# Products on a tile of ones around the first scores, queries scaled by immediates, and a later first output-weight block

## The chip, the cores and the metric

The kernel runs on one core of a Trainium2 chip. The metric is the device time of one execution, in microseconds (us). Before the change it is 948.71 us, the median of three runs (946.57 to 950.64).

## What is computed

Three layers, one after the other. First, attention over 4 batches of 8 heads, 576 positions, 64 values a head, with a causal window of 128 and a slope for each head:

```python
scores = scale * np.matmul(q, k.transpose(0, 1, 3, 2))
mask = (rel >= 0) & (rel < window)
scores = np.where(mask, scores + bias[None], -1000000000.0)
scores = scores - np.max(scores, axis=-1, keepdims=True)
attn = np.exp(scores)
attn = attn / (np.sum(attn, axis=-1, keepdims=True) + 1e-09)
attn_out = np.matmul(attn, v)
```

Its output, laid out as 2304 tokens of 512 values, goes through a gated layer of width 1536 (`silu(x @ w_gate) * (x @ w_val) @ w_out`) and then through a layer of width 2048 (`h * tanh(softplus(h)) @ w_out`, with `h = x @ w_in`).

## The kernel before

The 2304 tokens are cut into five chunks (512, 384, 512, 512, 384; `A_CHUNKS`). Attention of chunk c+1 is woven into the gated layer of chunk c; attention of chunk 0 stands alone, at the start. The last layer runs after all of that, with weights in seven combinations, and is not touched.

Only TensorE's order is written out by hand (`tc.manual_schedule(engines={PE})`): it is the order in which the program makes its calls. The order on VectorE (DVE), ScalarE (ACT), GpSimd (POOL) and on the DMA queue (SP) is made by a scheduler from its own estimates, so an edit in one place can move instructions of these engines far from it.

In chunk 0 a head h goes through these steps. **S(h)**, the scores (`score`, `mm` at L116): four products of queries by keys for the four blocks of 128 queries, two in each of two PSUM banks. They take 64 rows of the array, float32, and the profile shows each product as two instructions. DVE then puts the two diagonal halves together (L231, L238), adds the bias and takes the maximum (L245), and ACT takes exponentials and their sums (L249). `norm` adds a small number to the sums (L257), takes reciprocals (L260) and scales the weights, two blocks on ACT (L264) and two on DVE (L266). **T(h)**, four transposes (L271), which ACT copies (L277) and POOL masks (L280, L284). **O(r)**, for the pair r of heads 2r and 2r+1: weights by values into a bank, of which ACT and DVE make a high and a low part (L123, L126). The scores of a pair need its queries scaled first (`split`, L195: one ACT instruction for both heads, with a column of the constants `cst_sb` as scale).

TensorE's order is S(0), S(1), S(2), T(0), S(3), T(1), S(4), O(0), T(2), S(5) and so on. Scores, transposes, outputs and the hidden products `g_ps` of the gated layer take turns in four PSUM banks (tag `rot`); a product waits until the reader of the bank's last content is done.

Weights come as 64-bit patterns and are converted on the chip. `stage_w1(i)` loads raw block i of the first gated weight (tile `wst`, 1 MB; w0, w1, w2, ... below), `stage_other` raw block r of the output weight (tile `wraw`, 1 MB, one buffer; o0, o1, o2 below). `convert` makes five steps of each: one on ACT (`cg`, L434) and four on DVE (`cw` L446, `cp` L439, L451, L460). A w block is then split into halves, one on ACT (L123) and one on DVE (L126). These steps lie in a list, and `pump` hands them out between the pieces of attention. The first loads are issued in the order of `CFG["early"]`, where "w0", "w1", "w2" stand for the three entries of `stages`.

The gated layer of chunk 0 begins inside the attention (`begin`), and goes on after O(3): for block i a gate product and a tanh (L686, ACT), a product on DVE (L687), a value product, and h(i) (L697, DVE).

Of the kernel before, what the change touches and what calls it, by code (L numbers as in the profile page):

```python
# [9 lines left out]
F32 = mybir.dt.float32  # L10
F32R = mybir.dt.float32r
BF16 = mybir.dt.bfloat16
# [3 lines left out]
AF = mybir.ActivationFunctionType  # L16
# [5 lines left out]
F1, F2 = 1536, 2048  # L22
NF1, NF2 = F1 // 128, F2 // 128
W = 128
PLAIN = 3
CT = DM // 128
A_CHUNKS = [512, 384, 512, 512, 384]
# [66 lines left out]
def body(ctx: ExitStack, tc: tile.TileContext, qT, kT, vP, w1, w1o, w2, cst, yT):  # L94
# [20 lines left out]
    def mm(out, lhsT, rhs, start, stop):  # L115
        nc.tensor.matmul(out=out, lhsT=lhsT, rhs=rhs, start=start, stop=stop, skip_group_check=True)  # L116
# [12 lines left out]
    t = 0  # L129
# [2 lines left out]
        t += n  # L132


    x_t = {}

    def attention(ap, p, ci, s_native, upfront):
# [52 lines left out]
        def split(h):  # L190
            c = -float(2.0 ** (h - 2))
            if s_full(h):
                if h % 2 == 0:
                    q, k = raw.pop(h)
                    nc.scalar.activation(out=q, in_=q, func=AF.Copy, scale=qsc[:, h // 2:h // 2 + 1])  # L195
                    for e in range(2):
                        qk[h + e] = (q[64 * e:64 * e + 64], k[64 * e:64 * e + 64])
                return
            q, k = raw.pop(h)
            Q = ap.tile([128, p.n], F32R, tag="Q", name="Q")  # L200
            K1 = ap.tile([128, p.nk], F32R, tag="K1", name="K1")
            KL = ap.tile([128, p.nk], F32R, tag="KL", name="KL")
            nc.scalar.activation(out=Q, in_=q, func=AF.Copy, scale=c)
            hi_act(K1, k)
            nc.vector.scalar_tensor_tensor(
                out=Q[64:128], in0=q[64:128], scalar=c, in1=Q[64:128].bitcast(F32), op0=ALU.mult, op1=ALU.subtract
            )
            lo_dve(KL, k, K1)
            qk[h] = (Q, K1, KL)
# [105 lines left out]
    def attention_pieces(atts):  # L315

        heads = [(a, h) for a in atts for h in range(H)]
        pairs = [(a, r) for a in atts for r in range(HP)]
        n = len(heads)
        out = []  # L320

        def run(k, f):
            a, h = heads[k]
            return getattr(a, f)(h)

        def load(k):
            if not heads[k][0].upfront:
                run(k, "load")

        def load_v(r):  # L330
            if not pairs[r][0].upfront:
                pairs[r][0].load_v(pairs[r][1])

        def first():
            if atts[0].upfront:
                for c, i in ((x[0], int(x[1])) for x in CFG["early"]):
                    {"q": lambda: run(2 * i, "load"), "v": lambda: atts[0].load_v(i), "w": lambda: early[i]()}[c]()
            load(0)
            load_v(0)
            run(0, "split")  # L340
            load(1)
            load_v(1)

        def s_piece(k, g):
            a, h = heads[k]

            def f():
                if k == 0 and g == 0:
                    first()
                a.score(h, g)  # L350
                if g == a.ns - 1:
                    a.norm(h)
                    if k + 1 < n:
                        run(k + 1, "split")
                        if k + 2 < n:
                            load(k + 2)

            return (a.ci, 1.7 if a.s_full(h) else 0.87, f)

        def o_piece(k):  # L360
            a, h = heads[k]

            def f():
                if a.ci not in x_t:
                    x_t[a.ci] = xp.tile([128, 2, CT, 512], F32R, tag="x", name="xt")
                a.outp(h // 2)
                r = a.ci * HP + h // 2 + 2
                if r < len(pairs):
                    load_v(r)

            return (a.ci, a.nk * 0.46, f)

        def t_piece(k):
            a, h = heads[k]
            apart = 2.6 if h == H - 1 and a.ci == len(plansA) - 1 else 0.0
            return (a.ci, 0.48 + apart, lambda: a.transp(h))

        def delay(k):
            return CFG["delay0"] if heads[k][0].ci == 0 else 1

        for st in range(n + 4):
            todo = {"S": [], "T": [], "O": []}
            if st < n:
                todo["S"] = [s_piece(st, g) for g in range(heads[st][0].ns)]
            for k in range(max(0, st - 4), min(st, n)):
                if k + delay(k) == st:
                    todo["T"].append(t_piece(k))
                if k + delay(k) + 1 == st and heads[k][1] % 2 == 1:
                    todo["O"].append(o_piece(k))
            for c in CFG["order"]:  # L390
                if todo[c]:
                    out.append(todo[c].pop(0))
            for c in "SOT":
                out += todo[c]
        out.sort(key=lambda x: x[0] > 0)
        return out
# [88 lines left out]
    def stage_w1(i):  # L485
        stage[i] = (wp if i in (0, 1, 4, 5) else wq).tile([128, 2048], I32, tag="w", name="wst")
        nc.sync.dma_start(out=stage[i], in_=w1[i].bitcast(I32))

    def stage_other(key, src):
        stage[key] = bpool["a"].tile([128, 2048], I32, tag="wraw", name="wraw", bufs=1)  # L490
        nc.sync.dma_start(out=stage[key], in_=src.bitcast(I32))

    def conv_w1(i):
        st = {}

        def put(w):
            wt[i] = w
            stage.pop(i)
            if i + 4 < NF1:
                stage_w1(i + 4)  # L500

        def w_tile():
            return (wp if i < NF1 // 2 else wq).tile([128, 2, 1024], F32R, tag="w", name="w")

        steps(("w", i), convert(stage[i], st) + halves(st, w_tile, put))
# [480 lines left out]
    with tc.manual_schedule(engines={mybir.EngineType.PE}):  # L986
        spare = hp_.tile([128, 512], F32, tag="t", name="spare")[:, :1]
        nc.vector.memset(spare, 0.0)
        nc.scalar.activation(out=spare, in_=spare, func=AF.Exp)
        last = len(plansA) - 1  # L990
        att = tc.tile_pool(name="att", bufs=1, side="right")
        ap0 = att.__enter__()
# [19 lines left out]
        pieces = collections.deque(pieces)  # L1012
        lasts = [max(j for j, x in enumerate(pieces) if x[0] == ci) + 1 for ci in range(len(plansA))]
        at = 0
        stages = [lambda: stage_w1(0), lambda: stage_other(("o", 0), w1o[0]), lambda: stage_w1(1)]
        early.update(enumerate(stages))
        while at < lasts[0]:
            pieces.popleft()[2]()
            at += 1
            if at == 1:  # L1020
                conv_w1(0)
                conv_ring(0)
                conv_w1(1)
                nst = len(bg)
                stage_w1(2)
                stage_w1(3)
                behind.extend([last_of["max"], last_of["sum"]])
            if at == 4:
                behind.clear()
            f = (at / lasts[0] - CFG["conv_a"]) / (CFG["conv_b"] - CFG["conv_a"])  # L1030
            while bg and nst - len(bg) < f * nst:
                pump(1)
# [142 lines left out]
```

## Time and profile before

| | us |
|---|---|
| median of 3 runs | 948.71 |
| lowest, highest | 946.57, 950.64 |
| profiled execution, own time | 945.47 |
| profiled execution, span | 943.7 |
| TensorE busy | 919.4 |
| DVE busy | 701.4 |
| ACT busy | 519.7 |
| POOL busy | 204.7 |

A timeline row gives the start, the time from the first start to the last end of the merged instructions, the engine, the line, the operation, what it writes and reads, and how many instructions were merged; in brackets how long the engine stood idle before and what ended that. Matmuls of one row overlap, so a row's time divided by its count is the spacing. "PEclk" is the granted TensorE clock as a share of full speed; its record begins 42 us into the span, and before that the column shows full speed whatever was granted, so there the level is read from the spacing of the products.

### The profile page before, as it was taken

How to read it: one execution, taken by the hardware profiler on the slowest of the kernel's cores; microseconds unless marked ns; L12 is line 12 of the kernel's file. 1: busy time of each engine (PE TensorE's matmuls, PEld its weight loads, DVE VectorE, ACT ScalarE, POOL GpSimd, SP SyncE). 2: the span in 40 equal slices, each digit the busy share in tenths (PEclk: the TensorE clock that was granted, in tenths of full speed). 3: DMA queues.
4: the chain of work that ended last, by engine and by line, in shares of the span. 5: the costliest groups of instructions: out<-in, count | busy, mean ns of one | idle time of the engine just before them, and what ended most of it. 6: DMA issues, size and time to landing. Idle time of an engine off the chain costs nothing. (4 is left out here: it accounts for less than half of the span.)

```text
span 943.7 us, 14543 instructions
## 1 busy us (share of the span) xinstructions
PE 919.4 (97%) x5016; PEld 820.6 (87%) x5016; DVE 701.4 (74%) x1333; ACT 519.7 (55%) x1127; POOL 204.7 (22%) x332
## 2 busy tenths in 40 slices
PE   5999999999999999999999999999999999999998
PEld 4766678999988888888888999999999999999997
DVE  6898996687866865567665986887977878777673
ACT  6865667666575655445534554554535545355442
POOL 1312231111210332010013345551013410131000
PEclk9999999999999999999999999999999999999999
DMA  9855443376636464175437985426792267930375
GB/s 350 288 216 180 145 130 99 106 223 196 212 110 203 157 193 128 47 211 160 156 123 277 381 288 213 185 68 221 242 311 96 67 200 252 311 108 1 112 260 185
DMA packets 76729, 174.86 MB, mean 185 GB/s; under 512 B 8944, under 2 KB 52336, under 8 KB 66928
## 3 DMA queue, kind: packets, MB, share of 16 engines
q1 hardware_dynamic: 76512, 173.67, 55.3%
q8 instruction: 40, 0.66, 0.3%
q14 instruction: 33, 0.27, 0.1%
q10 hardware_dynamic: 144, 0.26, 0.1%
HBM read 138.25 MB, written 35.65 MB: 184 GB/s over the span
## 5 line engine op out<-in xcount | busy, mean ns | idle before, releaser
L116 PE MATMUL g_ps<-xt,w 128*128 128x512 f32 (+1 forms) x1440 | 318.3, 373 | 0.0
L116 PEld LDWEIGHTS g_ps<-xt,w 128*128 128x128 f32 x1440 | 257.6, 188 | 36.7 <-issue 3.5
L116 PE MATMUL bk<-xs,win 128*128 128x384 f32 x1008 | 177.9, 335 | 4.9 <-DVE G L759 4.6
L116 PEld LDWEIGHTS bk<-xs,win 128*128 128x128 f32 x1008 | 174.6, 188 | 7.8 <-DVE G L759 7.2
L116 PE MATMUL bk<-op,wout 128*128 128x384 f32 x1008 | 175.9, 334 | 1.3 <-DMA wout<-w2o 1.3
L116 PEld LDWEIGHTS bk<-op,wout 128*128 128x128 f32 x1008 | 174.7, 188 | 2.0 <-issue 2.0
L116 PE MATMUL acc<-hh,ring 128*128 128x512 f32 (+1 forms) x432 | 132.2, 369 | 0.0
L123 ACT ACTIVATE op<-G 128x768 fp32r<-128x768 f32 x84 | 71.0, 846 | 64.9 <-PE bk L116 64.8
L126 DVE TENSOR_TENSOR op<-G,op 128x768 fp32r<-128x768 f32 x84 | 80.2, 959 | 26.9 <-ACT op L123 24.9
L280 POOL TENSOR_SCALAR_AFFINE_SELECT PT<-PT 128x256 f32<-128x256 f32 (+4 forms) x80 | 43.2, 555 | 229.9 <-ACT PT L277 229.7
L850 POOL TENSOR_TENSOR t<-w 128x256 f32<-128x256 f32 x48 | 44.6, 950 | 210.1 <-issue 113.9
L116 PEld LDWEIGHTS acc<-hh,ring 128*128 128x128 f32 x432 | 80.0, 188 | 9.9 <-ACT hh L123 0.4
L116 PE MATMUL acc<-hl,ring 128*128 128x512 f32 (+1 forms) x216 | 79.0, 366 | 0.0
L249 ACT ACTIVATE Pt<-Pt,sm 128x128 f32<-128x128 f32 (+1 forms) x160 | 62.4, 391 | 16.1 <-DVE sm L245 15.7
L759 DVE TENSOR_TENSOR G<-u,bk 128x384 f32<-128x384 f32 x72 | 39.1, 553 | 36.6 <-PE bk L116 35.7
L1119 ACT ACTIVATE G<-G 128x384 f32<-128x384 f32 x72 | 37.0, 521 | 48.9 <-DVE G L759 48.9
L686 ACT ACTIVATE t<-g_ps 128x512 f32<-128x512 f32 (+1 forms) x60 | 32.9, 548 | 45.2 <-PE g_ps L116 45.1
L123 ACT ACTIVATE hh<-t 128x512 fp32r<-128x512 f32 (+1 forms) x54 | 31.2, 579 | 44.2 <-DVE t L702 44.0
L687 DVE SCALAR_TENSOR_TENSOR t<-t,g_ps 128x512 f32<-128x512 f32 (+1 forms) x60 | 37.6, 627 | 23.8 <-ACT t L686 23.7
L264 ACT ACTIVATE Pt<-Pt,sm 128x128 f32<-128x128 f32 (+1 forms) x144 | 46.3, 391 | 10.3 <-DVE sm L260 10.1
L126 DVE TENSOR_TENSOR hl<-t,hh 128x512 fp32r<-128x512 f32 (+1 forms) x54 | 36.6, 677 | 16.0 <-ACT hh L123 15.2
L759 DVE TENSOR_TENSOR G<-G 128x768 f32<-128x768 f32 x48 | 47.5, 990 | 0.8
(84 smaller groups left out, 1259.6 us busy)
## 6 DMA issues: line engine op xcount, KB each, us to landing
wout<-w2o SPq DMA_DIRECT2D x42, 1024.0 KB, 6.6
wraw<-w SPq DMA_DIRECT2D x16, 1024.0 KB, 5.5
w2o<-chl SPq DMA_DIRECT2D x16, 896.0 KB, 8.3
wst<-w SPq DMA_DIRECT2D x12, 1024.0 KB, 7.9
cw<-w1od SPq DMA_DIRECT2D x24, 512.0 KB, 4.5
w<-w2d SPq DMA_DIRECT2D x24, 512.0 KB, 3.3
w2d<-cw SPq DMA_DIRECT2D x16, 512.0 KB, 4.6
wraw<-w1o SPq DMA_DIRECT2D x6, 1024.0 KB, 6.9
```

The lines of the kernel that those rows point to most:

```text
L116: nc.tensor.matmul(out=out, lhsT=lhsT, rhs=rhs, start=start, stop=stop, skip_group_check=True)
L123: return nc.scalar.activation(out=out, in_=in_, func=AF.Copy)
L126: return nc.vector.tensor_tensor(out=out, in0=in_, in1=hi.bitcast(F32), op=ALU.subtract)
L249: last_of["sum"] = nc.scalar.activation(out=Pt[:q.qn], in_=Pt[:q.qn], func=AF.Exp, scale=-1.0, bias=sm[:q.qn, i:i + 1], accum_out=sm[:q.qn ...
L264: last_of["exp"] = nc.scalar.activation(out=pt, in_=pt, func=AF.Copy, scale=r)
L280: nc.gpsimd.affine_select(out=here, in_=prev, pattern=[[0, m], [1, n]], compare_op=ALU.is_ge, fill=0.0, base=0, channel_multiplier=-1,)
L686: tanhs.append(nc.scalar.activation(out=t[:, :n], in_=st["g"][:, :n], func=AF.Tanh, scale=0.5))
L687: nc.vector.scalar_tensor_tensor(out=t[:, :n], in0=t[:, :n], scalar=1.0, in1=st["g"][:, :n], op0=ALU.add, op1=ALU.mult)
L759: nc.vector.tensor_tensor(out=out, in0=a, in1=b, op=op)
L850: nc.gpsimd.tensor_tensor(out=x[:, o], in0=a, in1=b, op=ALU.subtract)
L1119: nc.scalar.activation(out=out, in_=in_, func=AF.Mish)
```

## The change

Four edits:

1. `runup(n)` issues n products of a 128x128 piece of a tile of bfloat16 ones by 128x512 of it, into the bank of tag `acc0`; nothing reads the result. 12 stand ahead of all scores, 4 behind the scores of each of heads 0, 1 and 2 (`RUNUP`). The tile is filled by one DVE memset.
2. The queries of heads 0 and 1 are scaled by constants written into the instructions: head 0's half on ACT, head 1's half on DVE, without the tile of constants.
3. In the early loads, w1 and o0 change places.
4. In the list of conversion steps, w1 comes ahead of o0.

```diff
+RUNUP = [12, 4, 4, 4]
...
+    def runup(n):
+        if not run:
+            t = hp_.tile([128, 512], F32, tag="t", name="ones")
+            run["one"] = t.bitcast(BF16)[:, :512]
+            nc.vector.memset(run["one"], 1.0)
+        spare = ps.tile([128, 512], F32, tag="acc0", name="spare", bufs=1)
+        for _ in range(n):
+            mm(spare, run["one"][:, :128], run["one"], True, True)
...
-                    nc.scalar.activation(out=q, in_=q, func=AF.Copy, scale=qsc[:, h // 2:h // 2 + 1])
+                    if upfront and h == 0:
+                        nc.scalar.activation(out=q[:64], in_=q[:64], func=AF.Copy, scale=c)
+                        nc.vector.tensor_scalar(out=q[64:], in0=q[64:], scalar1=2 * c, scalar2=None, op0=ALU.mult)
+                    else:
+                        nc.scalar.activation(out=q, in_=q, func=AF.Copy, scale=qsc[:, h // 2:h // 2 + 1])
...
                 a.score(h, g)
+                if g == a.ns - 1 and k + 1 < len(RUNUP):
+                    runup(RUNUP[k + 1])
...
         nc.scalar.activation(out=spare, in_=spare, func=AF.Exp)
+        runup(RUNUP[0])
...
-        stages = [lambda: stage_w1(0), lambda: stage_other(("o", 0), w1o[0]), lambda: stage_w1(1)]
+        stages = [lambda: stage_w1(0), lambda: stage_w1(1), lambda: stage_other(("o", 0), w1o[0])]
...
                 conv_w1(0)
+                conv_w1(1)
                 conv_ring(0)
-                conv_w1(1)
```

What moves is shown below as each kernel's rows, with the numbers of its tiles; line numbers in the changed kernel are its own, 12 to 18 higher.

On TensorE, around S(0) and S(1) of the changed kernel (`s_ps_128` and `s_ps_146` are S(0), `s_ps_169` and `s_ps_183` S(1)):

```order
L117 MATMUL s_ps_128<-qkv_103 128x256 x2
L117 MATMUL s_ps_146<-qkv_103 128x256
L117 MATMUL s_ps_146<-qkv_103 128x128
L117 LDWEIGHTS ones_85
L117 MATMUL spare_156<-ones_85 128x512
...
L117 MATMUL s_ps_169<-qkv_103 128x256 x2
L117 MATMUL s_ps_183<-qkv_103 128x256
L117 MATMUL s_ps_183<-qkv_103 128x128
```

Before, S(1) follows S(0) directly; now four products on ones, each with a weight load, stand between them.

On ACT, from the first conversion of w0 to the scaling of head 0's weights, before (`wst_92` is w0, `w_218` its half, `sm_113` the sums of head 0, `sm_149` those of head 1):

```order
L434 ACTIVATE cg_128<-wst_92 128x1024
L195 ACTIVATE qkv_98<-qkv_98,cst_sb_79 128x512
L249 ACTIVATE Pt_134,sm_113<-Pt_134,sm_113 128x128
...
L249 ACTIVATE Pt_157,sm_149<-Pt_157,sm_149 128x128
L123 ACTIVATE w_218<-cw_160 128x1024
L249 ACTIVATE Pt_166,sm_149<-Pt_166,sm_149 128x128
L264 ACTIVATE Pt_137<-Pt_137,sm_113 128x128
```

And in the changed kernel, from the same place to the first scaling of head 1 (`wst_107` is w0, `wst_116` w1, `w_249` and `w_387` their halves, `wraw_123` o0, `sm_129` and `sm_170` the sums of heads 0 and 1):

```order
L452 ACTIVATE cg_144<-wst_107 128x1024
...
L265 ACTIVATE Pt_178,sm_170<-Pt_178,sm_170 128x128
L452 ACTIVATE cg_292<-wst_116 128x1024
L124 ACTIVATE w_249<-cw_181 128x1024
...
L280 ACTIVATE Pt_153<-Pt_153,sm_129 128x128
...
L452 ACTIVATE cg_437<-wraw_123 128x1024
...
L124 ACTIVATE w_387<-cw_336 128x1024
L280 ACTIVATE Pt_190<-Pt_190,sm_170 128x128
```

The conversion step of w1 and the half of w1 have moved ahead of the scaling of head 1's weights; the former also ahead of head 0's. Before, both stood behind them.

On ACT, at the first tanh instructions of the gated layer, before (`t_590`, `t_632` and `t_676` are blocks 0, 1 and 2; `wraw_636` is o2):

```order
L686 ACTIVATE t_590<-g_ps_459 128x512
L686 ACTIVATE t_632<-g_ps_473 128x512
L434 ACTIVATE cg_770<-wraw_636 128x1024
L686 ACTIVATE t_676<-g_ps_663 128x512
L123 ACTIVATE w_680<-cw_660 128x1024
```

and in the changed kernel (`t_621`, `t_663`, `t_707`; `wraw_667` is o2):

```order
L704 ACTIVATE t_621<-g_ps_491 128x512
L452 ACTIVATE cg_801<-wraw_667 128x1024
L704 ACTIVATE t_663<-g_ps_499 128x512
L704 ACTIVATE t_707<-g_ps_694 128x512
L124 ACTIVATE w_711<-cw_691 128x1024
```

The conversion step of o2 has moved ahead of the tanh of block 1. On DVE, the instruction that reads that tanh (L687 before, L705 now) stands ahead of the maxima of head 8 (the first head of chunk 1) in both kernels; in the changed one it stands behind h(0) instead of ahead of it.

## Rows read from the trace of the kernel before

**Rows 1.** The page: busy time, share of the span and instructions of each engine.

```profile
PE 919.4 (97%) x5016; PEld 820.6 (87%) x5016; DVE 701.4 (74%) x1333; ACT 519.7 (55%) x1127; POOL 204.7 (22%) x332
```

**Rows 2.** Stretches: length, busy us of PE, PEld, DVE, ACT, POOL, clock, DMA.

```profile
8.30:26.50 18.20, 14.29 (x45) 10.43 (x43) 18.11 (x65) 15.26 (x47) 4.54 (x6) 1.00 1.05 379
31.00:62.00 31.00, 31.00 (x164) 22.34 (x163) 26.83 (x72) 21.24 (x56) 10.62 (x16) 1.00 0.83 308
72.00:110.00 38.00, 38.00 (x156) 23.71 (x156) 35.33 (x67) 23.16 (x53) 10.43 (x22) 1.00 0.48 166
```

**Rows 3.** Timeline of PE, 0 to 72 us: S, T, O, hidden products.

```profile
6.24 7.21 PE L116 MATMUL s_ps<-qkv 64*128 64x256 f32 x24 [6.24 <-ACT qkv L195]
...
21.31 0.77 PE L271 MATMUL t_ps<-cst_sb,Pt 128*128 128x128 f32 x2 [1.10 <-ACT Pt L264]
22.61 0.69 PE L271 MATMUL t_ps<-cst_sb,Pt 128*128 128x128 f32 x2 [0.53 <-DVE Pt L266]
23.22 3.35 PE L116 MATMUL s_ps<-qkv 64*128 64x256 f32 x8
26.50 3.25 PE L116 MATMUL o_ps<-PT,qkv 128*64 128x256 f32 x16
...
33.11 1.78 PE L116 MATMUL s_ps<-qkv 64*128 64x256 f32 x8
34.82 2.25 PE L116 MATMUL o_ps<-PT,qkv 128*64 128x256 f32 x16
...
39.71 3.00 PE L116 MATMUL g_ps<-xt,w 128*128 128x512 f32 x12
...
63.13 0.92 PE L116 MATMUL s_ps<-k,q 64*64 64x192 f32 x4 [1.07 <-DVE sm L245]
...
71.42 0.88 PE L271 MATMUL t_ps<-cst_sb,Pt 128*128 128x128 f32 x4 [0.97 <-ACT Pt L264]
```

**Rows 4.** Timeline of ACT, 5 to 62 us.

```profile
5.47 0.72 ACT L195 ACTIVATE qkv<-qkv,cst_sb 128x512 f32<-128x512 f32 x1 [2.74 <-DMA cst_sb<-cst]
...
10.00 1.11 ACT L434 ACTIVATE cg<-wst 128x1024 bf16<-128x1024 bf16 x1
...
13.94 1.06 ACT L123 ACTIVATE w<-cw 128x1024 fp32r<-128x1024 f32 x1 [0.41 <-DVE cw L460]
...
20.09 0.40 ACT L249 ACTIVATE Pt<-Pt,sm 128x128 f32<-128x128 f32 x1 [0.84 <-DVE sm L245]
...
20.87 0.68 ACT L264 ACTIVATE Pt<-Pt,sm 128x128 f32<-128x128 f32 x2
...
57.35 0.60 ACT L686 ACTIVATE t<-g_ps 128x512 f32<-128x512 f32 x1 [1.88 <-PE g_ps L116]
60.89 1.13 ACT L434 ACTIVATE cg<-wraw 128x1024 bf16<-128x1024 bf16 x1 [2.94 <-DMA wraw<-w1o]
```

**Rows 5.** Timeline of DVE, 8 to 63 us.

```profile
8.35 0.43 DVE L231 COPY_PREDICATED s_ps<-cst_sb,s_ps 128x256 f32<-128x256 uint8 x1 [7.42 <-PE s_ps L116]
...
11.93 0.42 DVE L439 TENSOR_SCALAR cp<-cg 128x512 int32<-128x512 int32 x1
...
59.96 0.67 DVE L687 SCALAR_TENSOR_TENSOR t<-t,g_ps 128x512 f32<-128x512 f32 x1
60.56 0.67 DVE L697 SCALAR_TENSOR_TENSOR h<-t,g_ps 128x512 f32<-128x512 f32 x1
...
62.49 0.28 DVE L245 CUSTOM_DVE_ANT_0 Pt<-s_ps,cst_sb 128x128 f32<-128x128 f32 x1
```

**Rows 6.** Issue of o0's load (last: start) and its time to landing.

```profile
L491 SPq DMA_DIRECT2D wraw<-w1o x1: 441/441/441, 5.3 to 5.3; - x1
...
DMA to landing us min/median/max: 8.8/8.8/8.8
```

**Rows 7.** Issue of w1's load and its time to landing.

```profile
L487 SPq DMA_DIRECT2D wst<-w x1: 894/894/894, 10.2 to 10.2; - x1
...
DMA to landing us min/median/max: 9.5/9.5/9.5
```

More of the change, by code (lines that the diff above doesn't have):

```diff
@@ L132, in body @@
         t += n
+    run = {}
+    def runup(n):
[6 more added lines that the diff above has]
+            mm(spare, run["one"][:, :128], run["one"], True, True)
     x_t = {}
```

## The prediction

> **What bounds the kernel now.** I read four views in this order. The page first: TensorE is busy in 97% of the span [rows 1]. So a change can move the time only where TensorE stands still, or runs slowly. The stretches next: from 31 to 62 us and from 72 to 110 us TensorE has no gap at all [rows 2]; a delay that enters either stretch leaves it unchanged, and the change touches nothing behind. What counts is therefore what happens before 31 us, and between 62 and 72.
>
> TensorE's timeline shows both places [rows 3]. Before 31 us it starts at 6.24, waits for ACT and DVE at T(1), and runs at the lower of its two levels: S(4), from 23.22, takes 3.35 us for 8 instructions, S(6), from 33.11, 1.78 for the same, half of it. That is 1.2 and 2.4 GHz. O(0) took 3.25, O(1) 2.25. At 62 us it waits 1.07 for a maximum of DVE before the second half of S(9), and at 71.42 it waits 0.97 for ACT [rows 3].
>
> The timelines of ACT and DVE say why. From 8.3 to 26.5 us DVE is busy for 18.11 of 18.20 us [rows 2]: DVE and ACT set the pace there, not TensorE. ACT follows its list strictly, and waits where it meets something that has not landed.
>
> **The change part by part.**
>
> *Products ahead of S(0), and the queries.* No row shows a bfloat16 product of 512 columns. The nearest is the hidden product, 12 in 3.00 us, 0.25 each [rows 3], at the upper level; at the lower I double it. Twelve take 3.0 to 6.0 us, from about 1.5 (the memset cannot take longer than the 128x512 instruction of 0.42 [rows 5], and DVE has nothing else then). They end between 4.5 and 7.5; I take 6.0, half of them slow. The queries are no longer held up by the constants (ACT waited for them until 5.47 [rows 4]), but behind the products that gains next to nothing, and DVE's half of the scaling lies in its idle time before 8.35 [rows 5]. So S(0) starts near 6.0 instead of 6.24. If the level is up by then, DVE's first score instruction comes about 2.1/2 us later, near 7.1 instead of 8.35 [rows 5]: a head start of 1.2 us for DVE.
>
> *What becomes of the head start.* DVE's `cp` of w0, at 11.93 [rows 5], needs ACT's `cg` of w0, at 10.00 for 1.11 us [rows 4], which stands behind the second pair's queries and does not move. DVE waits there until 11.2: 0.7 us of the head start is left.
>
> *The products behind S(0), S(1), S(2).* 4 x 0.25 is 1.0 us each, 3.0 in all, 6.0 at the lower level. They also end something: S(0) to S(2), 24 instructions, took 7.21 us [rows 3], though 8 at 0.42 are 3.35; two heads ran side by side on the two halves of the array, which a product of the whole array between them forbids. At the upper level: 3 x 1.78 + 3.0 = 8.3 us, from 6.0 to 14.3. The cover is T(0), which cannot come before ACT has scaled head 0, after 16 us (below). I cost them at nothing; without this cover they would cost their 3.0 us.
>
> *w1 ahead of o0.* This is the term that decides. Before, ACT was through with what it had at 13.94 - 0.41 = 13.53 [rows 4]. Now `cg` of w1 stands there. w1 lands where o0 landed, at 5.3 + 8.8 = 14.1 [rows 6]; both are 1 MB. `cg` ends at 14.1 + 1.11 = 15.2. From the half of w0 (13.94) to the scaling of head 1 (20.87) ACT took 6.93 us, 0.84 of it waiting [rows 4], so 6.1 of work. That list now also holds the half of w1, 1.06 like that of w0, and a wait of some 0.3 for o0, which lands where w1 did, at 10.2 + 9.5 = 19.7 [rows 7]. Sum: 15.2 + 6.1 + 1.1 + 0.3 = 22.7, 1.8 later than 20.87. T(1) follows by 0.4, at 23.1. Before, T(1) began at 21.31 and S(4) at 23.22, with a wait of 0.53 for DVE's scaling in between [rows 3]; DVE, ahead by 0.7 and no longer holding up T(1), takes that wait away, and so S(4) comes at 23.1 + 1.91 - 0.53 = 24.5 at the latest, with tighter transposes 24.1. I take 24.2: **+1.0 us**. Bounds: 0, if ACT's estimate is off by its slack, and +1.3.
>
> *The level from T(0) on.* S(0) to S(2) were 7.21 us without a break, and S(4) was still slow; the level rose behind O(0), and S(6) is fast [rows 3]. In the changed kernel the products end near 14 and TensorE then waits for ACT until 16 to 17. I take S(4) and O(0) as slow as before, so the 1.0 stays. The other end is both fast: 1.57 + 1.0 = 2.6 us less.
>
> No row shows the level fall, since TensorE never waits long after 31 us. [...]
>
> *The tanh of block 1 behind o2.* Before, it ran at 57.35; then ACT waited 2.94 us for o2 and converted it at 60.89 [rows 4]. Now the conversion stands first. About as many bytes lie ahead of o2 as before, so I take the same landing, 60.8. Conversion to 62.0, tanh (0.60) to 62.6. DVE's L687 of block 1, before at 59.96, waits for that. From its start to head 8's first maximum at 62.49 went 2.53 us, with h(0), 0.60 (60.56 to the next), in it [rows 5]; h(0) now goes before. So the maximum comes at 62.6 + 1.9 = 64.5 and S(9), 0.64 behind it as before, at 65.2 instead of 63.13 [rows 3]: **+2.0 us**, which takes in the 1.0 from above. T(8) at 71.42 hangs on exponentials of the same maxima [rows 3], so its wait absorbs nothing. Ends: a landing before 59 us leaves +1.0, one 1.3 later +3.3.
>
> *Sum.* +2.0 us on the profiled execution: 945.47 + 2.0 = 947.5. That execution lies 3.2 below the median of the runs, 948.71, so the median becomes **950.7 us**.
>
> **The rivals.**
>
> *The level stays up, and o2 lands early.* S(4) from 24.2 and O(0) at the fast rows end at 24.2 + 1.78 + 2.25 = 28.2 instead of 26.50 + 3.25 = 29.75: -1.5, median 947.2. For it: the products raise the level sooner than the program does. Against: DVE is full up to 26.5 [rows 2]. Chance 0.15.
>
> *o2 lands early alone.* Only the +1.0: 949.7. For it: ACT shows only when the last part of that load came, and it waited there for 2.94 us [rows 4]. Chance 0.22.
>
> *The level never rises* (slower). The mechanism sits between S(0) and T(0): from 7.5 us, S(0) to S(2) one after another take 3 x 3.35 and the products 6.0, to 23.5; T(0), S(3) and T(1) follow with 1.3, 3.35 and 1.3, and S(4) begins at 29.4 instead of 23.22, +6.2. If a slow product costs 0.43 (as much as 256 float32 columns in one instruction) and not 0.50, and S keeps 3.0, it is +3.1. Middle +4.6: 953.3. It decides as soon as S(1) runs at 0.42 an instruction. Chance 0.12.
>
> *o2 lands later*, behind a store that moved ahead of it: +3.3, 952.0. Chance 0.13.
>
> **How the numbers follow.** The forecast, 950.7, has 0.38. The range 946.0 to 953.6 reaches from the first rival less a microsecond of the runs' own spread (946.57 to 950.64) to the middle of the slow rival. 0.5% is 4.7 us, about what a measurement of this kernel can tell from no change: 944.0 to 953.5. Faster by more than that needs the first rival and 3 us besides: 0.05. Slower has the upper half of the slow rival and the tails of two others: 0.11. Within it: 0.84.
>
> **What would show it.** Right: S(0) near 6 and instructions of S(1) at 0.21; ACT idle before `cg` of w1 until 14.1; T(1) near 23 and S(4) near 24.2, at 0.42 an instruction; the tanh of block 1 behind 62; a gap of some 2 us before S(9). Wrong: S(4) before 23.2, or O(0) at the fast spacing; S(9) at or before 63.1.

## The result, and the profile after

The changed kernel takes **955.11 us**, the median of 8 runs (951.49 to 959.14). Before, in 8 runs of the same measurement, it took 948.05 us (946.57 to 950.64). The ratio of the runs is 1.008, with a 95% interval of 1.0063 to 1.0097 (the two medians alone give 1.0074): slower by 0.8%, 7.1 us, more than the 4.7 us that can be told from no change. The prediction was +2.0 us, 950.7, with a range to 953.6, and "no change" with a chance of 0.84. It was wrong in size and in its likeliest class. One of the twelve runs of experiment 3 below took 1842 us, twice as long as the others, and is left out of its ratio.

The profiled execution took 955.4 us, with a span of 953.4, close to its median. The one before had 945.47, some 2.6 below its median; so the two profiles lie 9.9 us apart, and 7.1 of that is the difference of the medians.

The page's line of busy time, against [rows 1], and the first two stretches of [rows 2] in the changed kernel:

```profile
PE 928.0 (97%) x5040; PEld 822.3 (86%) x5040; DVE 701.3 (74%) x1335; ACT 519.9 (55%) x1127; POOL 205.9 (22%) x332
```

```profile
8.30:26.50 18.20, 14.82 (x53) 9.81 (x52) 18.06 (x64) 15.64 (x45) 4.52 (x6) 0.75 1.05 379
31.00:62.00 31.00, 27.05 (x142) 19.22 (x142) 19.33 (x64) 19.93 (x55) 9.63 (x17) 0.89 0.84 293
```

TensorE is busy for 8.6 us more, which is about what the 24 products took (5.30 us for twelve, 1.04 for each four behind), nearly all of it where it would have waited. DVE, ACT and POOL have the work that they had. The second stretch is the find: TensorE had no gap there before [rows 2], and now is busy for 27.05 of 31.00 us, at a mean clock of 0.89. That is where the time went.

The clock column can be read in both of these stretches: in the changed kernel's trace the record of the clock begins some 7 us into the span. In the kernel before it begins some 31 us into the span, where S(5) turns fast, and not at 42, as was said ahead of the prediction; 42 is the trace's own count, which starts 11 us ahead of the span.

TensorE's timeline of the changed kernel, the rows that answer to [rows 3] (T is L287 now, the maximum L261):

```profile
1.55 5.30 PE L117 MATMUL spare<-ones 128*128 128x512 bf16 x12 [1.55 <-DVE ones L142]
6.78 1.91 PE L117 MATMUL s_ps<-qkv 64*128 64x256 f32 x8
...
17.22 1.19 PE L287 MATMUL t_ps<-cst_sb,Pt 128*128 128x128 f32 x4 [2.21 <-ACT Pt L280]
18.35 3.35 PE L117 MATMUL s_ps<-qkv 64*128 64x256 f32 x8
22.88 1.20 PE L287 MATMUL t_ps<-cst_sb,Pt 128*128 128x128 f32 x4 [1.18 <-ACT Pt L280]
24.00 3.35 PE L117 MATMUL s_ps<-qkv 64*128 64x256 f32 x8
27.28 3.69 PE L117 MATMUL o_ps<-PT,qkv 128*64 128x256 f32 x16
...
33.80 1.78 PE L117 MATMUL s_ps<-qkv 64*128 64x256 f32 x8
35.51 0.65 PE L117 MATMUL o_ps<-PT,qkv 128*64 128x256 f32 x2
40.10 3.25 PE L117 MATMUL o_ps<-PT,qkv 128*64 128x256 f32 x14 [3.95 <-POOL PT L300]
43.28 1.12 PE L287 MATMUL t_ps<-cst_sb,Pt 128*128 128x128 f32 x4
...
46.58 3.01 PE L117 MATMUL g_ps<-xt,w 128*128 128x512 f32 x12
...
69.91 0.92 PE L117 MATMUL s_ps<-k,q 64*64 64x192 f32 x4 [1.07 <-DVE sm L261]
...
78.21 0.89 PE L287 MATMUL t_ps<-cst_sb,Pt 128*128 128x128 f32 x4 [0.98 <-ACT Pt L280]
```

Up to 34 us it is the forecast: T(1) at 22.88 (forecast 23.1), S(4) at 24.00 (24.2), S(6) at 33.80, 0.7 later than before [rows 3]. Then O(1) begins at 35.51, issues two instructions, and stops for 3.95 us, until POOL has masked the weights of head 3. The 14 that are left take 3.25 us (1.73 at the upper level, experiment 4), T(4) 1.12 and not 0.65. The first hidden products begin at 46.58 instead of 39.71 [rows 3], 6.9 late, and nothing is won back: S(9)'s second half comes at 69.91 (63.13 before) and T(8) at 78.21 (71.42), 6.8 late each, behind the same waits of 1.07 and 0.98.

Who held up the masks? ACT's timeline (L211 is the scaling of queries, L280 that of weights, L293 the copy of transposes, L452 `cg`, L704 the tanh):

```profile
14.03 1.14 ACT L452 ACTIVATE cg<-wst 128x1024 bf16<-128x1024 bf16 x1 [0.57 <-DMA wst<-w]
...
36.58 0.61 ACT L211 ACTIVATE q<-q,cst_sb 128x384 f32<-128x384 f32 x1 [3.14 <-DMA q<-qT]
...
37.48 0.68 ACT L280 ACTIVATE Pt<-Pt,sm 128x128 f32<-128x128 f32 x2
38.06 0.58 ACT L293 ACTIVATE PT<-t_ps 128x512 f32<-128x512 f32 x1
...
64.07 1.15 ACT L452 ACTIVATE cg<-wraw 128x1024 bf16<-128x1024 bf16 x1 [1.81 <-DMA wraw<-w1o]
65.12 0.58 ACT L704 ACTIVATE t<-g_ps 128x512 f32<-128x512 f32 x1
```

And POOL's two masks of head 3:

```profile
38.71 0.63 POOL L296 TENSOR_SCALAR_AFFINE_SELECT PT<-PT 128x512 f32<-128x512 f32 x1 [0.39 <-ACT PT L293]
39.41 0.64 POOL L300 TENSOR_SCALAR_AFFINE_SELECT PT<-PT 128x512 f32<-128x512 f32 x1
```

At 33.4 us ACT meets the scaling of the queries of chunk 1's second pair, heads 10 and 11, whose scores come some 40 us later. Their load has not landed: ACT stands still for 3.14 us. Its second piece had not even been issued; the DMA queue came to that at 33.81, and it took 2.7 us from there (its row, and the time to landing of that issue):

```profile
33.81 0.43 SPq L177 DMA_DIRECT2D q<-qT  x1
DMA to landing us min/median/max: 2.7/2.7/2.7
```

So the early place of the row makes the wait, and not a load that is slow. Behind the row, in ACT's list, lie head 5's first exponential, the scaling of head 4's weights (37.48) and T(3)'s copy (38.06), for which POOL waits, and for POOL O(1). Before, the same copy stood behind T(2)'s with one exponential between them, ran at 33.28, and the queries' scaling came at 41.70, when they were there (the second piece of their load was issued at 35.9 and landed 5.3 us later):

```profile
33.28 0.60 ACT L277 ACTIVATE PT<-t_ps 128x512 f32<-128x512 f32 x1 [0.54 <-PE t_ps L271]
...
41.70 0.60 ACT L195 ACTIVATE q<-q,cst_sb 128x384 f32<-128x384 f32 x1
```

In ACT's order the queries' scaling and T(3)'s copy stand like this, before and after (`PT_312` and `PT_343` are T(2)'s copies, `PT_353` and `PT_383` T(3)'s):

```
before                                       after
L277 ACTIVATE PT_312<-t_ps_307               L293 ACTIVATE PT_343<-t_ps_338
L249 ACTIVATE Pt_284,sm_264 (head 4)         L265 ACTIVATE Pt_315,sm_295 (head 4)
L277 ACTIVATE PT_353<-t_ps_348  T(3)         L211 ACTIVATE q32_652  chunk 1, pair 1
L249 ACTIVATE Pt_323,sm_318 (head 5)         L265 ACTIVATE Pt_354,sm_349 (head 5)
                                             L280 ACTIVATE Pt_315, Pt_300 (head 4)
                                             L293 ACTIVATE PT_383<-t_ps_378  T(3)
```

### The profile page after: what moved, and what is told of

Read it like the earlier page. It is cut to its first block, busy times and chain, and to the rows that moved or that the text cites. A ratio compares the mean times of both kernels' runs of the same rounds, so it can differ in the third digit from the quotient of the medians.

```text
span 953.4 us, 14586 instructions
## 1 busy us (share of the span) xinstructions
PE 928.0 (97%) x5040; PEld 822.3 (86%) x5040; DVE 701.3 (74%) x1335; ACT 519.9 (55%) x1127; POOL 205.9 (22%) x332
## 5 line engine op out<-in xcount | busy, mean ns | idle before, releaser
L296 POOL TENSOR_SCALAR_AFFINE_SELECT PT<-PT 128x256 f32<-128x256 f32 (+4 forms) x80 | 47.3, 608 | 233.1 <-ACT PT L293 233.0
L704 ACT ACTIVATE t<-g_ps 128x512 f32<-128x512 f32 (+1 forms) x60 | 32.8, 546 | 47.2 <-PE g_ps L117 47.1
L705 DVE SCALAR_TENSOR_TENSOR t<-t,g_ps 128x512 f32<-128x512 f32 (+1 forms) x60 | 37.5, 626 | 25.1 <-ACT t L704 25.1
L280 ACT ACTIVATE Pt<-Pt,sm 128x128 f32<-128x128 f32 (+1 forms) x144 | 46.3, 390 | 11.8 <-DVE sm L276 11.5
```

Of the source, the lines that this page charges most:

```text
L280: last_of["exp"] = nc.scalar.activation(out=pt, in_=pt, func=AF.Copy, scale=r)
L296: nc.gpsimd.affine_select(out=here, in_=prev, pattern=[[0, m], [1, n]], compare_op=ALU.is_ge, fill=0.0, base=0, channel_multiplier=-1,)
L704: tanhs.append(nc.scalar.activation(out=t[:, :n], in_=st["g"][:, :n], func=AF.Tanh, scale=0.5))
L705: nc.vector.scalar_tensor_tensor(out=t[:, :n], in0=t[:, :n], scalar=1.0, in1=st["g"][:, :n], op0=ALU.add, op1=ALU.mult)
```

## The experiments

**Theory.** The loss is the place of that row: ACT waits for a load ahead of T(3)'s copy, and TensorE then runs O(1) and T(4) at the lower level. **Rivals.** The products cost it, or the clock by itself; w1 ahead of o0 costs it by ACT's wait for w1; the wait would only move elsewhere. The table puts the fourteen runs together. "g_ps" is the begin of the first hidden products, "S(9)" that of the second half of S(9), "T(8)" that of T(8), all from TensorE's timelines; the ratio is to the runs of before in the same measurement, as recorded, and differs from the quotient of the two medians by up to 0.0011. The times are of one execution each, and not always a typical one: those of experiments 8, 10 and 3 took 5.5, 3.0 and 2.5 us more than the median of their kernel.

| kernel | g_ps | S(9) | T(8) | ratio (95%) |
|---|---|---|---|---|
| before | 39.71 | 63.13 | 71.42 | 1 |
| changed | 46.58 | 69.91 | 78.21 | 1.0080 (1.0063 to 1.0097) |
| 1: row behind T(5)'s copy | 42.80 | 66.12 | 74.41 | 1.0023 (1.0005 to 1.0042) |
| 2: edits 1, 2 alone | 39.84 | 64.92 | 73.22 | 1.0015 (0.9996 to 1.0033) |
| 3: the same, waits filled | 38.69 | 63.35 | 73.07 | 1.0027 (1.0006 to 1.0048) |
| 4: changed, O(1)'s wait filled | 46.26 | 69.57 | 77.87 | 1.0068 (1.0050 to 1.0086) |
| 5: edits 3, 4 alone | 40.45 | 64.04 | 72.33 | 1.0009 (0.9996 to 1.0022) |
| 6: changed without edit 3 | 44.69 | 70.03 | 78.32 | 1.0067 (1.0045 to 1.0089) |
| 7: before, T(3)'s copy late | 42.56 | 65.98 | 74.27 | 1.0044 (1.0028 to 1.0060) |
| 8: before, two waits filled | 45.40 | 68.72 | 77.02 | 1.0028 (1.0010 to 1.0047) |
| 9: changed without the first 12 | 41.73 | 65.05 | 73.34 | 1.0027 (1.0009 to 1.0044) |
| 10: queries loaded early | 42.13 | 66.81 | 77.25 | 1.0029 (1.0013 to 1.0045) |
| 11: as 8, and ahead of O(0) | 39.19 | 63.14 | 71.44 | 0.9993 (0.9979 to 1.0007) |
| 12: edit 2 alone | 38.73 | 62.50 | 70.91 | 1.0001 (0.9985 to 1.0018) |
| 13: as 1, O(1)'s wait filled | 41.11 | 65.30 | 73.59 | 1.0040 (1.0026 to 1.0054) |
| 14: 11 and 12 together | 38.05 | 61.73 | 73.39 | 1.0049 (1.0031 to 1.0067) |

**1. The row tied behind T(5)'s copy.** Everything on TensorE and SP stays as in the changed kernel; on ACT that one row moves, and a few rows of ACT and DVE for heads 8 and 9 change places, some 50 rows on.

```diff
-                        nc.scalar.activation(out=q, in_=q, func=AF.Copy, scale=qsc[:, h // 2:h // 2 + 1])
+                        with (tc.issue_after(last_of["t5"].ins) if ci == 1 and h == 2 else ExitStack()): nc.scalar.activation(out=q, in_=q, func=AF.Copy, scale=qsc[:, h // 2:h // 2 + 1])
...
-            pt_[h] = pt.rearrange("p s c -> p (s c)")
+            pt_[h] = pt.rearrange("p s c -> p (s c)"); last_of.setdefault(f"t{h}", last_of["act"])
```

> The changed kernel, with one row of ACT moved: the scaling of the queries of chunk 1's second pair is tied behind T(5)'s copy (it stood ahead of T(3)'s copy). Theory (the order of that one row carries the loss): T(3)'s copy comes near 34 us, O(1) begins near 35.5 and does not stop, takes 2.25 us and not 3.25, and g_ps of the first block begins near 40.4 (46.58 in the changed kernel, 39.71 before); the median is 948 to 949.5, a ratio to before of 1.000 to 1.002. Rival A (products on ones, or the level of the clock, carry it): the median stays at 955. Rival B (the wait moves to another reader of the same bank or buffer): 951 to 953.

949.65 us, ratio 1.0023, just above my range: of the 0.8% some 0.57 are gone with one row. What is left shows in ACT and TensorE:

```profile
34.77 0.57 ACT L293 ACTIVATE PT<-t_ps 128x512 f32<-128x512 f32 x1
...
44.37 0.60 ACT L211 ACTIVATE q<-q,cst_sb 128x384 f32<-128x384 f32 x1
```

```profile
35.21 0.65 PE L117 MATMUL o_ps<-PT,qkv 128*64 128x256 f32 x2
36.80 3.12 PE L117 MATMUL o_ps<-PT,qkv 128*64 128x256 f32 x14 [0.94 <-POOL PT L300]
```

The wait for the queries is gone, but T(3)'s copy comes at 34.77, not 33.28: the exponential of head 5 and the scaling of head 4 still stand ahead of it. O(1) stops for 0.94 us, and its 14 instructions are slow again. The theory held for the wait and was too small for the order: three other rows had moved ahead of the copy as well.

**2. Edits 1 and 2 alone** (edits 3 and 4 undone).

> Edits 1 and 2 alone (products on ones, queries scaled by immediates); loads and conversion steps in the order of before. Theory (the loss comes from the order that edits 3 and 4 bring about): ACT's scaling of chunk 1's second pair stays behind T(4)'s copy, O(1) does not stop, the median is 947 to 949, ratio 0.999 to 1.002. Rival A (products carry the loss): 953 to 955. Rival C (products gain if w1 does not hold up ACT): 945 to 946.5.

949.09 us, ratio 1.0015, its interval on both sides of 1. The row stays behind T(4)'s copy, and O(1) does not stop. The products alone do not bring the loss. ACT waits for the same load here too, but with T(3)'s copy long done:

```profile
40.84 0.62 ACT L211 ACTIVATE q<-q,cst_sb 128x384 f32<-128x384 f32 x1 [1.98 <-DMA q<-qT]
```

What stands behind it is T(5)'s copy, and O(2) stops for 1.14 us. **5. Edits 3 and 4 alone** (no products, the column as scale):

> Edits 3 and 4 alone (w1 ahead of o0 in the loads and in the list); no products, queries scaled by the column of constants. In this kernel T(3)'s copy stands right behind T(2)'s on ACT, and the scaling of chunk 1's second pair behind T(4)'s copy. Theory (what costs is T(3)'s copy behind that scaling, which only all edits together bring about): O(1) does not stop for over 0.6 us, median 946.5 to 949, ratio 1.000 to 1.002. Rival A (w1 ahead of o0 costs by itself, through ACT's wait for w1): T(1) near 23, 949.5 to 951. Rival B (edits 3 and 4 bring the whole loss): 953 to 955.

946.52 us, ratio 1.0009. T(1) at 21.08 is where it was, and g_ps 0.7 late; the row stands behind T(4)'s copy, and ACT waits for 1.23 us there. So neither pair of edits brings the loss. Among these kernels the scheduler puts the row that early only where products meet edit 4; edit 3 is not needed for most of the loss, as experiment 6 shows. (T(1) near 23 in the changed kernel is no work of w1 alone either; in experiment 2 it is at 22.11.)

**9. The changed kernel without the 12 products ahead** (`RUNUP = [0, 4, 4, 4]`).

> The changed kernel without the 12 products ahead of S(0); the 4 behind S(0), S(1) and S(2), the immediates and edits 3 and 4 stay. With them left out, ACT's order has T(3)'s copy four rows earlier (ahead of head 4's scaling) and the scaling of chunk 1's second pair behind T(4)'s copy. Theory (the 12 products cost nothing on TensorE, and everything through the order that they bring ACT to): O(1) does not stop for over 0.6 us, median 1 to 2.5 us over before at most, ratio 0.999 to 1.0025. Rival (the loss is in edits 3 and 4, or in the products behind the scores): ratio 1.005 to 1.008.

949.14 us, ratio 1.0027, just above the upper end that I gave the theory, far under the rival's. O(1) does not stop, and the row is back behind T(4)'s copy, so the row moves only where the 12 products are there. That g_ps comes 2.0 us late has another cause, most likely the one that TensorE's timeline shows:

```profile
8.33 1.89 PE L117 MATMUL spare<-ones 128*128 128x512 bf16 x4
10.15 3.35 PE L117 MATMUL s_ps<-qkv 64*128 64x256 f32 x8
...
20.22 1.06 PE L289 MATMUL t_ps<-cst_sb,Pt 128*128 128x128 f32 x4
```

The four products behind a head's scores take 1.89 us here, and a head's scores 3.35: the lower level, from 5.05 to beyond 20 us, though TensorE never stood still for long. That is the mechanism of the slow rival, in the kernel without its run-up: T(0) at 20.22 instead of 15.73. The 12 products did buy something, then: a level at which the other 12 are cheap.

**6. The changed kernel with the loads in the old order** (edit 3 undone). In this order the row stands one place behind T(3)'s copy.

> The changed kernel with edit 3 undone: loads in the order of before, conversion steps of w1 still ahead of o0 in the list. ACT then has T(3)'s copy right behind T(2)'s, and the scaling of chunk 1's second pair just behind T(3)'s copy instead of ahead of it. Theory (the wait hurts by what stands behind it): ACT waits for those queries as in the changed kernel, to 36 us or later, but O(1) does not stop for over 0.6 us; the wait now holds up T(4)'s copy by 0 to 2 us; median 948 to 951. Rival (the early wait costs the same wherever it stands): 953 to 955.

952.19 us, ratio 1.0067: between my range and the rival's, nearer the rival's (six runs, from 947.79 to 954.43). I was wrong about what stands behind the wait.

```profile
37.78 0.61 ACT L211 ACTIVATE q<-q,cst_sb 128x384 f32<-128x384 f32 x1 [5.35 <-DMA q<-qT]
```

```profile
34.14 0.89 PE L117 MATMUL s_ps<-qkv 64*128 64x256 f32 x4 [1.34 <-DVE sm L261]
...
39.51 1.20 PE L287 MATMUL t_ps<-cst_sb,Pt 128*128 128x128 f32 x4 [1.68 <-ACT Pt L280]
```

ACT waits for 5.35 us. O(1) gets its masks, but S(6)'s second half waits 1.34 us for a maximum of DVE and T(4) 1.68 for ACT's scaling, which stands behind the row; S(7) then takes 3.35 us, at the lower level. So the row costs in this place as well, by other rows behind it. **10. The load early instead** (the second pair's queries loaded next to the first pair's; its scaling stands even further ahead of T(3)'s copy) turns this around:

```diff
-    if k + 2 < n:
+    if k + 2 < n and k + 2 != 10:
         load(k + 2)
+    if k == 5:
+        load(10)
```

> The changed kernel with the loads of chunk 1's second pair issued next to those of the first, ahead of w4. Its scaling on ACT stays ahead of T(3)'s copy (seven rows ahead of it). Theory (the wait for the load is the cost, the place of the row only its condition): ACT does not wait there for over 0.5 us; T(3)'s copy comes near 35, behind head 4's scaling; O(1) stops for about 1 us and is slow, as in the run with the row tied behind T(5)'s copy; ratio to before 1.0015 to 1.004. Rival A (no wait, no loss at all): 0.999 to 1.001. Rival B (place, not load): 1.006 to 1.009.

949.44 us, ratio 1.0029. ACT waits for 0.84 us at that row, at 28.26, and O(1) stops for 0.94 as in experiment 1:

```profile
28.26 0.62 ACT L211 ACTIVATE q<-q,cst_sb 128x384 f32<-128x384 f32 x1 [0.84 <-DMA q<-qT]
```

```profile
36.15 3.25 PE L117 MATMUL o_ps<-PT,qkv 128*64 128x256 f32 x14 [0.94 <-POOL PT L300]
```

Two ways to take the same wait away, a later row and an earlier load, give the same time. The wait for the load is the cause of the larger part, 0.5 to 0.6% of the 0.8%.

**7. The rest put into the kernel before.** T(3)'s copy there is tied behind head 5's exponentials and head 4's scaling, six rows, with no other edit (chunk 1's second pair tied behind T(5)'s copy, where it was).

> The kernel before, with T(3)'s copy on ACT tied behind the exponentials of head 5 and the scaling of head 4 (six rows, 2.6 us of ACT), and chunk 1's second pair kept behind T(5)'s copy. No other edit. Theory (T(3)'s chain of copy, masks and O(1) has no slack in the kernel before): T(3)'s masks end near 37.5, O(1) stops for 1.5 to 2.5 us, TensorE falls to the lower level for the rest of O(1) and T(4); in all 2.5 to 4.5 us by g_ps of the first block, median 2 to 4.5 above before, ratio 1.002 to 1.005. Rival (DVE sets the pace from 40 to 63 us and takes in a delay of this size): ratio 0.999 to 1.001.

949.2 us, ratio 1.0044. One row says it:

```profile
36.79 3.13 PE L116 MATMUL o_ps<-PT,qkv 128*64 128x256 f32 x14 [2.01 <-POOL sm L216]
```

A copy later by 1.4 us (34.69, before 33.28) stops O(1) for 2.01, and the 14 instructions are slow (3.13, at the upper level 1.73). From O(1)'s begin to g_ps it takes 8.43 us instead of 4.89 [rows 3]. This execution began S(0) 0.5 us earlier than the one before; what is left, 2.85 us at g_ps, is still 2.85 at S(9) and at T(8): nothing is taken in on the way. T(3), its copy, its masks and O(1) have no slack in the kernel before. Its own rows say so: O(1) began at 34.82 [rows 3], while POOL's second mask, which its third instruction needs, ended only at 35.29:

```profile
34.65 0.64 POOL L284 TENSOR_SCALAR_AFFINE_SELECT PT<-PT 128x512 f32<-128x512 f32 x1
```

**4. O(1)'s wait filled** in the changed kernel, with 18 products on ones ahead of O(1).

> The changed kernel with 18 products on ones ahead of O(1), where TensorE stood still for 3.95 us. ACT's order stays as in the changed kernel, so O(1) begins as late, near 40. Theory (of the 6.8 us some 1.5 to 1.9 are the level that fell in that wait): O(1) takes 2.25 us and not 3.25, T(4) 0.65 and not 1.12, and the median is 953.2 to 953.8, 1.5 below the changed kernel. Rival (the level has no part, only the wait): 955, or over it if 18 products are longer than the wait.

953.93 us, ratio 1.0068. Here the load was issued later, its second piece at 35.5, and ACT waited for 5.54 us, until 38.36; TensorE:

```profile
41.89 1.73 PE L117 MATMUL o_ps<-PT,qkv 128*64 128x256 f32 x14 [2.37 <-POOL PT L300]
43.55 0.66 PE L287 MATMUL t_ps<-cst_sb,Pt 128*128 128x128 f32 x4
```

O(1) began 1.8 us later than in the changed kernel, and was fast: 1.73 and 0.66. So by the rows the level was worth about 2 us of the 6.8 there, the 1.5 of 3.25 - 1.73 and the 0.5 of T(4). The times of the runs do not show it: the intervals of the two ratios overlap. **13. The same for experiment 1**, with 6 products:

> The changed kernel with its one row of ACT tied behind T(5)'s copy, and 6 products on ones (1.3 us) ahead of O(1), where TensorE stopped for 0.94 us in that run and fell to the lower level for O(1) and part of T(4). Theory (the 3 us left over in that run are 0.7 from T(1), 0.9 of wait and 1.4 of lower level): O(1) begins near 36.7, takes 1.73 to 2.0 us for its 16 instructions, g_ps of the first block begins at 41.3 to 41.7 (42.80 without the products), ratio 1.000 to 1.0015. Rival (the level has no part in what reaches the end): ratio 1.002 to 1.003 as without them.

g_ps begins at 41.11, 1.7 earlier than in experiment 1, as the theory has it. But the ratio is 1.0040, not below 1.0023: above the theory's range and the rival's. ACT and TensorE show what took half of the 1.7 back:

```profile
61.07 1.14 ACT L454 ACTIVATE cg<-wraw 128x1024 bf16<-128x1024 bf16 x1 [4.30 <-DMA wraw<-w1o]
62.10 0.59 ACT L706 ACTIVATE t<-g_ps 128x512 f32<-128x512 f32 x1
```

```profile
65.30 0.92 PE L117 MATMUL s_ps<-k,q 64*64 64x192 f32 x4 [1.94 <-DVE sm L261]
```

ACT waits for o2's load until 61.0, the tanh of block 1 follows at 62.10, and S(9) waits for 1.94 us, until 65.30. That is the last step of the prediction to the tenth (tanh 62.0 to 62.6, S(9) at 65.2), in a kernel that arrives there early enough to meet it. At T(8) 2.2 us are left of the loss, 0.8 less than in experiment 1. Why the runs are not faster than experiment 1's is not shown; the two intervals overlap.

**3, 8, 11, 12, 14. Can the useful parts be had without the loss?** Experiment 3 fills the waits ahead of T(0) and T(1) in experiment 2 (14 and 12 products); 8 does so in the kernel before (6 and 10, no others); 11 adds 8 products ahead of O(0); 12 is edit 2 alone; 14 is 11 and 12.

> As the run with edits 1 and 2 alone, with 14 products behind S(2) instead of 4, and 12 behind S(3), to fill the waits in which TensorE fell to the lower level. Theory (the level falls in those waits, and S(3), S(4) and O(0) are slow for that alone): S(3), S(4) take 1.78 us, O(0) 2.25, and of the 1.57 + 1.00 us some 1.5 to 2.6 reach the end: the median is 945.5 to 947, ratio 0.997 to 0.999. Rival (DVE and ACT set the pace up to 26 us): S(4) and O(0) are fast, and TensorE waits for what they save; the median is that of edits 1 and 2 alone within 0.7 us.

> The kernel before with 6 products on ones behind S(2) and 10 behind S(3), nothing else. Theory (S(4) and O(0) are slow only for the level, and the waits before T(0) and T(1) are where it is lost): if the level is up by 23 us, S(4) takes 1.78 and O(0) 2.25 us, g_ps of the first block begins 1 us earlier, and DVE at S(9) takes back part of it: ratio 0.998 to 1.000. Rival A (S(0) to S(2) never raise the level, and 6 products are too few): products 0.43 apart, S(4) at 3.35, ratio 1.000 to 1.002.

> As the run with 6 products behind S(2) and 10 behind S(3), with 8 more ahead of O(0), where TensorE waited for POOL there and fell to the lower level until 42 us. Theory (that fall was the loss): O(0), S(5), S(6) and O(1) at the upper level, g_ps of the first block at 38.5 to 39.5 us (39.71 before, 45.40 in that run), ratio 0.998 to 1.000 and a narrower spread of runs. Rival (DVE at S(9) takes back what is gained before 55 us): g_ps early, S(9) at 63 or later, ratio 1.000 to 1.002.

> Edit 2 alone: queries of heads 0 and 1 scaled by immediates, half on DVE; no products, loads and list as before. Theory: S(0) up to 0.7 us earlier, as it no longer waits for the constants; DVE and ACT carry up to 0.5 us of that to T(1); DVE at S(9) decides what is left: ratio 0.999 to 1.000. Rival (ACT's order moves against it): 1.001 to 1.004.

> The kernel before with edit 2 (immediates) and products on ones only in the waits: 6 behind S(2), 10 behind S(3), 8 ahead of O(0). It puts together the two kernels that lay nearest below the one before. Theory (each gives up to 0.6 us of its own by 55 us): g_ps of the first block near 38.2, S(9) near 62.5, ratio 0.998 to 0.9995. Rival (DVE at S(9) decides): S(9) at 63, ratio 0.9995 to 1.001.

Experiment 11 came out as the theory had it in g_ps and ratio, and as the rival had it at S(9); 12 lies at the upper end of the theory's range; in 3, 8 and 14 the ratio lies above the theory's range, and in 8 and 14 above the rival's too. In 3 the level stayed up until past T(8) (S(3), S(4) 1.78 each), g_ps came 1.0 us early, and by T(8) 1.65 us were lost. In 8 S(4) was early and fast, so O(0) met the masks of POOL, and the level fell just there; it did not come back until 43 us (this execution is the slowest of the twelve):

```profile
27.32 3.25 PE L117 MATMUL o_ps<-PT,qkv 128*64 128x256 f32 x14 [1.82 <-POOL PT L302]
```

Products in that wait too (11) keep it up, and g_ps is at 39.19; S(9) and T(8) are where they were before, and the ratio is 0.9993. Edit 2 alone brings S(0) to 5.08, T(8) half a microsecond forward, and 1.0001. Both together are the earliest of all at g_ps and S(9), and lose 0.5%:

```profile
63.60 1.13 ACT L456 ACTIVATE cg<-wraw 128x1024 bf16<-128x1024 bf16 x1 [7.04 <-DMA wraw<-w1o]
```

```profile
73.39 1.17 PE L289 MATMUL t_ps<-cst_sb,Pt 128*128 128x128 f32 x4 [4.34 <-ACT Pt L282]
```

ACT waits for o2 for 7.04 us, everything behind it waits, T(8) stands still for 4.34 us, and TensorE runs S(10), 1.99 us for 4 instructions, and what follows at the lower level. None of these kernels is measurably faster than the one before.

No run puts T(3)'s copy back into its old place in the changed kernel. That what experiment 1 leaves comes from that copy's place, and from the 0.7 us of T(1), rests on experiment 7 and on rows.

## Why the prediction was wrong, point by point

- **Products ahead, queries.** The price was wrong: a slow product took 0.43 and not 0.50, but all 12 were slow, from 1.55 to 6.78; so S(0) came at 6.78, not near 6.0, and DVE's head start was 0.28 us (8.07 instead of 8.35), not 1.2. In the other seven executions with these 12 products S(0) came at 5.77 to 6.79, so the 6.0 lies within what differs from one to the next. It did not matter: what follows hung on ACT.
- **Products behind S(0) to S(2).** Right: 1.04 us each, at the upper level, covered by T(0), which waited for ACT until 17.22.
- **w1 ahead of o0.** Right in its numbers: w1 landed at 14.0 (forecast 14.1), `cg` at 14.03, T(1) at 22.88, S(4) at 24.00, +0.8 where 1.0 was forecast. Experiment 5 shows that the edit alone does not do it; the sum was right for the order that ACT had with the products.
- **The level from T(0) on.** Right in this execution: it fell behind the wait of 2.21 us ahead of T(0), and S(3), S(4) and O(0) were slow. It was less sure than it read: in experiment 10 a wait of 2.61 us in the same place left T(0) and most of S(3) fast (0.84 and 1.97 us). The Trainium skill, page "TensorE: Matmul & The Clock Gate", section "HAM oscillation — how this bites in real kernels", tells of a kernel in which waits for loads, some 3 to 5 us long, bring the lower level back every time. The waits here were shorter, so that case did not cover them, and the rows decide: the level fell behind 0.94 us (experiments 1 and 10), 2.01 (7) and 1.82 (8) as well, and stayed behind the 1.14 us ahead of O(2) in experiment 2.
- **The step that failed** is the first one, not a term: "a delay that enters either stretch leaves it unchanged, and the change touches nothing behind. What counts is therefore what happens before 31 us, and between 62 and 72." I read from TensorE's full row of 31 to 62 us that nothing could happen there. In its place the runs showed, inside that stretch, a wait of 3.95 us at O(1) and 2.2 us of lower level behind it, and TensorE came out of it 6.8 us late. A stretch without a gap has no idle time to lose; it says nothing of how near the next wait is. T(3)'s copy ended in time by nothing at all (experiment 7), and the order on ACT, which decides when that copy runs, is made anew for the whole program by an edit at its start. The changed kernel's order has the row ahead of T(3)'s copy, as shown above, and I priced only the rows near the edits. A sign was to be had: in the kernel before these queries landed at 41.2, long after T(2)'s copy (31.77), and in ACT's new order their row stands two places behind that copy.
- **The tanh behind o2** was forecast at +2.0 us at S(9). In the changed kernel the order is as forecast (64.07, then 65.12), and the cost is nothing, since TensorE arrives 6.8 us late: S(9) waits 1.07 as before. Experiment 13 shows the tanh and S(9) at their forecast times. So, as far as T(8), the forecast had the changed kernel without the early row about right: 2.2 us, for 2.0. The runs of experiment 13 are slower by more, 3.8 us by the medians, and what comes behind T(8) there is not explained.
- **The rival that the level never rises** gave 953.3, nearest to the result, by a mechanism that did not occur here (S(1) took 1.78 us for 8, the fast spacing): that is luck. Experiment 9 shows it in its own place, at some 2 us by g_ps instead of 4.6.

The account of the 6.8 us at g_ps: 0.7 came in with T(1); 3.95 is the wait at O(1); and 2.2 is what followed it, O(1), T(4) and the begin of S(7) at the lower level. The remaining difference between the two profiles, up to 953.4 - 943.7 = 9.7 us, comes behind 200 us, in waits that differ from run to run (for loads of the last layer's output weights 2.4 us in three waits, before 1.3 in two), and is mostly not in the medians.

## What to carry to other kernels

Where a scheduler orders the queues, price the change by its whole new order: look on each in-order engine for a row that has moved ahead of others and waits for a load, however far from the edit, and ask what is queued behind it, and when that load is issued. "No gap" on the bounding engine is not "slack": the chain that feeds it may be on time by nothing, and then a delay passes in full, while time that is won early is taken back at the next load or full engine. A wait of TensorE can have a second price, the lower clock behind it, which at O(1) was half as much again (2.2 us for 3.95).

## What the runs showed of the hardware that was not expected

**Whether the level falls behind a wait is not told by the length of the wait alone.** It fell behind 0.94 us at O(1) (experiments 1 and 10), and stayed behind 2.37 us at the same place in experiment 4, where products on ones had filled 3.8 us just before. Two microseconds with next to nothing on TensorE, first of the changed kernel, then of experiment 4 (columns as in [rows 2]; the clock is the third from the end):

```profile
38.00:40.00 2.00, 0.00 (x0) 0.00 (x0) 0.10 (x1) 2.00 (x10) 1.33 (x3) 0.50 1.05 356
```

```profile
40.00:42.00 2.00, 0.11 (x2) 0.11 (x4) 0.28 (x2) 2.00 (x10) 1.38 (x3) 1.00 1.04 369
```

**The same wait can go either way.** T(8) waits for some 0.98 us in most kernels. Before, in the changed kernel and in experiments 1, 12 and 13 the clock stays at 1.00 behind it. In experiments 2 and 11 it falls to 0.50 for 3.4 us, and 1.7 us are lost; in the profile of experiment 11:

```profile
70.00:72.00 2.00, 1.01 (x5) 0.31 (x4) 2.00 (x4) 1.97 (x5) 0.00 (x0) 1.00 0.22 41
74.00:76.00 2.00, 2.00 (x3) 0.67 (x2) 1.14 (x7) 1.29 (x6) 1.46 (x6) 0.50 0.31 123
```

Why it falls in one and not in the other is open; it may be one source of the spread between runs of one kernel, of which only one each was profiled.

**The same scores raised the level in one execution and not in another.** On TensorE experiments 8 and 11 are the same up to S(4): scores of three heads, two heads side by side, for some 7 us, and then 6 products on ones. In 8 the products are slow, in 11 fast from the first on:

```profile
12.90 2.74 PE L117 MATMUL spare<-ones 128*128 128x512 bf16 x6
```

```profile
12.47 1.47 PE L117 MATMUL spare<-ones 128*128 128x512 bf16 x6
```

So in 11 the scores alone had raised it, and in 8 they had not. In experiment 9, with four products between the heads' scores, TensorE went from 5.05 to over 20 us almost without a break at the lower level; in the changed kernel it ran the 12 products from 1.55 to 6.78 at the lower level, and S(1) behind them was fast. What decides it these runs do not tell. Products of 128x128 by 128x512 in bfloat16 followed each other at 0.216 us at the upper level and 0.427 at the lower (changed kernel).
